# Both triangles multiplied in one slot, two vector products and one transpose queued behind the state's sums

## The chip, the cores and the metric

The kernel runs on one core of a Trainium2 chip. A core has a matrix engine (TensorE; PE in the profile, with PEld for its weight loads), a vector engine (VectorE, DVE), a scalar engine (ScalarE, ACT), GpSimd (POOL) and SyncE (SP), whose queue here issues most transfers. Each engine works through its own list of instructions in order, and semaphores hold one until what it needs is done. The metric is the time of one execution on the device in microseconds.

## The reference, cut to what matters

Three stages follow each other: a recurrence over 768 steps for 4 x 8 heads of width 40, a plain two-layer network, and a mixture of 8 experts.

```python
for t in range(S):                                   # S = 768
    y[:, :, t] = einsum('bhd,bhde->bhe', rt, state)
    Sa = einsum('bhde,bhe->bhd', state, at)
    state = state * wt - outer(Sa, bt) + outer(vt, kt)
x = y as (3072, 320)
g = relu(x @ w_in) ** 2;  x = g @ w_out              # w_in 320 x 2048
expert = argmax(x @ w_gate)                          # 8 experts, capacity 768 each
out = gate * (relu(x_e @ w1_e) @ w2_e) put back by token
```

## The kernel before

The 768 steps are cut into 12 stages of 64 steps (`NS`), and each stage into two chunks of 32 steps (`NC`, c = 0 and 1). Within a chunk nothing is done step by step: the products of the chunk's rows of `a` with its columns of `k` and `b` form two lower triangles per head, one of them is inverted, and with the inverse the 32 steps become matrix products.

What is needed of a stage before the state reaches it is made one stage ahead:

- `scale` loads `w`, `k` and `b` (tile `kb_d`, one buffer) and `a`; a scan over the decays gives R (`rq_r`, L115), `k` and `b` are multiplied by it on DVE (L146, two instructions), a second scan (`rq_q`, L128) gives what `a` is multiplied with on POOL (L280, through `times`). `kb_d` can be loaded anew only when both `lower` calls have read it.
- `lower(s, c)` multiplies the triangles of chunk c on PE (tile `pa`, 64 small products), copies one out on ACT (`solve_ab`, L174), masks the other on DVE (`am`, L176) and turns it into place in `a` (L180).
- `invert` transposes `solve_ab` of both chunks into `solve_al` on DVE (L187). Then POOL inverts by elimination: a memset, two copies, and 31 pairs of a product into `tmp` and a difference in `solve_tl`, all L280, each waiting for the one before it. `inverted` transposes the result back (`solve_tf`, L207) and forms `tt` (L210, L211).
- `steps` runs the same two scans with another layout (`wl`); `over` (L122, ACT) reads that R, and its transposed pieces `rt` (L244, L245, two buffers, one for each chunk) are fetched by SP as `rx` (L265), with which `zk` is multiplied.

In a stage, chunk c does in turn: `right` (tile `pr`: `a` times the state `zv`), `solve` (tile `psa`: the inverse `tt` times that), `turn` and `inner` (`psd`, `ppq`), `mix` (`ppq` masked into `lr`, L369), and the state's sums: `step` adds the products `pn` to `zv` and `other` adds the products of the chunk before to `zk` (both in `update`, L296, on DVE). `zk` of the chunk before is finally multiplied by the decay `g_b` (L389), before `out` (tile `py`) reads it.

The plain network's products (`pl` L434, `acc` L616) and its elementwise work (`g`, `gh`, `gl`) for the tokens already finished are put between these, a fixed number of pieces after each slot. The experts' products follow the recurrence (`upl`, `uacc`).

The program is recorded slot by slot, and a scheduler then sets each engine's order. Products on PE are kept in the order in which they were recorded (`keep_in_program_order`); on DVE, ACT and SP the scheduler moves instructions freely where no dependence or `issue_after` forbids it. Slots of chunk 0 are a to g, of chunk 1 a, b, d, f, g. Before, the two triangles of the next stage stand in different slots, with the network's pieces and slot d between them:

```python
def slot_c():
    if more: rw.lower(s + 1, 0)
def slot_e():
    if more:
        rw.lower(s + 1, 1)
        rw.invert(s + 1)
        st = rw.steps(s + 1)
```

Of the kernel before, what the change touches and what calls it, by code (L numbers as in the profile page):

```python
# [16 lines left out]
ALU = mybir.AluOpType  # L17
# [20 lines left out]
ROWS = 64 + D  # L38
# [19 lines left out]
BY_COL = [slice((1 - j) * 64, (1 - j) * 64 + D) for j in range(2)]  # L58
# [3 lines left out]
class Rwkv:  # L62
# [6 lines left out]
    def __init__(self, ctx, tc, ps, consts, keep, wd, kb, ad, rv, wl, tok, rng):  # L69
        self.tc, self.nc, self.ps = tc, tc.nc, ps  # L70
        self.c = consts
        self.src = dict(wd=wd, kb=kb, ad=ad, rv=rv, wl=wl, tok=tok)
        nc = self.nc
        p1 = ctx.enter_context(tc.tile_pool(name="rw1", bufs=1))
        self.p = ctx.enter_context(tc.tile_pool(name="rwr", bufs=1))
        self.dram = ctx.enter_context(tc.tile_pool(name="rwdram", bufs=2, space=DRAM))
        self.sq = p1.tile([128, 16, SEG], F32, name="seed_q")
        self.w = keep.tile([128, 1 + 16 * SEG], F32, tag="w_d", name="w_d")
        self.kb = keep.tile([128, 2, 16, SC], F32, tag="kb_d", name="kb_d")
        self.gb = p1.tile([128, 16, D], F32, name="g_b")  # L80
# [12 lines left out]
        for t in (self.a[1][32:64, :, 1], *(t[32:64, 1] for t in self.zv + self.lr + self.zk), self.gb[32:64]):
            nc.gpsimd.memset(t, 0.0)
        for t in (self.zv[0], self.zk[0]):
            nc.gpsimd.memset(t[0:64, 1], 0.0)
            nc.gpsimd.memset(t[64:128, 0], 0.0)
        self.last = None
        self.pre, self.rt = {}, {}

    def psum(self, name):
# [31 lines left out]
    def scale(self, s):  # L133

        nc, src = self.nc, self.src
        w, kb, a = self.w, self.kb, self.a[s % 2]
        for j in range(2):
            nc.sync.dma_start(out=w[BY_COL[j]], in_=src["wd"][s, j])
        for j in range(2):
            nc.sync.dma_start(out=kb[BY_COL[j]], in_=src["kb"][s, j])  # L140

        pr = self.products(w, 16, ROWS, s)
        r = next(pr)
        yield
        for k in range(2):
            nc.vector.tensor_mul(kb[:ROWS, k], kb[:ROWS, k], r[:ROWS, :, 1:SEG])  # L146
            yield
        g = self.tile([128, 16], f"g64.{s}", 2)
        nc.vector.tensor_copy(g[:ROWS], r[:ROWS, :, 0])
        self.pre[s] = [g, [None] * NC, None]  # L150
        for j in range(2):
            nc.sync.dma_start(out=a[BY_COL[j], :, j].rearrange("p c n t -> p c (n t)"), in_=src["ad"][s, j])
        q = next(pr)
        yield
        for j in range(2):
            v = a[BY_COL[j], :, j]
            self.times(s == 0 and j == 0, out=v, in0=v, in1=q[BY_COL[j], :, 0:SC].rearrange("p n (c t) -> p c n t", c=NC))
        self.wl = self.tile([128, 1 + 10 * SEG], f"wl.{s}", 1)
        nc.sync.dma_start(out=self.wl, in_=src["wl"][s])
        yield  # L160
# [42 lines left out]
    def inverted(self, s):  # L203

        nc, tl = self.nc, self.tl
        tf = self.tile([128, C, 2, NC, H], f"solve.tf{s}", 2)
        nc.vector.transpose(out=tf.rearrange("p t u c h -> p (t u c h)"),  # L207
                            in_=tl[:, :, :, None].to_broadcast([128, C, C // 2, 2]))
        tt = self.tile([128, C, NC, H], f"tt.{s}", 2)
        nc.scalar.mul(tt, tf[:, :, 0], self.c["odd"][:, 0:1])  # L210
        i = nc.vector.scalar_tensor_tensor(out=tt, in0=tf[:, :, 1], scalar=self.c["odd"][:, 1:2], in1=tt,  # L211
                                           op0=ALU.mult, op1=ALU.add)
        self.pre[s][2] = tt
        return i.ins
# [33 lines left out]
    def fetch(self, s, c):  # L248
# [17 lines left out]
        for j in range(2):  # L266
            v = zk[BY_STEP[j], j].rearrange("p (h y) e -> p y h e", y=2)
            self.times(c == 1, out=v, in0=v, in1=rx[BY_STEP[j]])

    def times(self, fast, **k):  # L270

        if fast:
            self.nc.vector.tensor_tensor(op=ALU.mult, **k)
        else:
            self.pool(self.nc.gpsimd.tensor_tensor, op=ALU.mult, **k)
# [9 lines left out]
    def update(self, s, c, z, l, r, half):  # L285

        nc = self.nc
        pn = self.psum(f"pn{s}_{c}_{half}")[:, 0:8 * D].rearrange("p (n e) -> p n e", n=8)
        for n in range(8):
            i = half * 8 + n  # L290
            for j in range(2):
                rows = BY_STEP[j]
                self.mm(pn[BY_COL[j], n], lhsT=l[rows, j, i], rhs=r[rows, j, i], start=True, stop=True)
        for j in range(2):
            rows, ns = BY_COL[j], slice(half * 8, half * 8 + 8)
            nc.vector.tensor_tensor(out=z[c ^ 1][rows, j, ns], in0=z[c][rows, j, ns], in1=pn[rows], op=ALU.add)  # L296

    def right(self, s, c):

# [26 lines left out]

    def step(self, s, c, half):

        self.update(s, c, self.zv, self.zk[c], self.zv[c], half)

    def decay(self, s):

# [49 lines left out]

    def other(self, s, c, half):

        self.update(s, c, self.zk, self.zv[c], self.zk[c], half)
        if half == 1 and c == NC - 1 and s + 1 < NS:
            for j in range(2):
                v = self.zk[c ^ 1][BY_COL[j], j]
                self.nc.vector.tensor_mul(v, v, self.gb[BY_COL[j]])  # L389

# [930 lines left out]
def tile_rwkv__mlp__moe(ctx, tc, wd, kb, ad, rv, wl, tok, nat, w_in, w_out, w_gate, w1, w2, cap, cst1, cst2, out):  # L1323
    nc = tc.nc
# [8 lines left out]
    with ExitStack() as ph:  # L1333
# [4 lines left out]
        rw = Rwkv(rp, tc, ps, consts, keep, wd, kb, ad, rv, wl, tok, rng)  # L1338
# [48 lines left out]
        for s in range(NS):  # L1387
# [3 lines left out]
            for c in range(NC):  # L1391
                last, y = ys, None
# [25 lines left out]
                def slot_c():  # L1418
                    if s > 1:
                        pieces.append(ml.bursts(s - 1, xs.pop(s - 1)))  # L1420
                    if more:
                        rw.lower(s + 1, 0)

                def slot_d():
                    rw.turn(s, c)
                    rw.inner(s, c)

                def slot_e():
                    nonlocal st
                    if more:  # L1430
                        rw.lower(s + 1, 1)
                        rw.invert(s + 1)
                        st = rw.steps(s + 1)
                        next(st)

# [10 lines left out]
                def slot_g():  # L1446
                    rw.step(s, c, 0)
                    rw.step(s, c, 1)
                    if c == 1 and more:
                        rw.inverted(s + 1)  # L1450

                parts = slot_a, slot_b, slot_c, slot_d, slot_e, slot_f, slot_g
                if c == 1:
                    parts = slot_a, slot_b, slot_d, slot_f, slot_g
# [48 lines left out]
    n = nc.values_load(good[0:1, 0:1], min_val=0, max_val=128)  # L1503
# [86 lines left out]
```

## Time and profile before

| | us |
|---|---|
| median of 3 runs | 1195.83 (1195.64 to 1196.54) |
| the profiled execution | 1200.53 |
| its span in the trace | 1198.7 |
| recurrence, from the first chunk to the last sums | about 85 to 880 |
| experts | from about 880 to the end |

The profiled execution is one more execution, 4.70 us above the median; the trace covers its span, and 1.83 us lie around it. Times in the views are counted from the span's start. In a timeline row, square brackets give the engine's idle time just before the instruction and what ended it.

### The profile page before, as it was taken

How to read it: one execution, taken by the hardware profiler on the slowest of the kernel's cores; microseconds unless marked ns; L12 is line 12 of the kernel's file. 1: busy time of each engine (PE TensorE's matmuls, PEld its weight loads, DVE VectorE, ACT ScalarE, POOL GpSimd, SP SyncE). 2: the span in 40 equal slices, each digit the busy share in tenths (PEclk: the TensorE clock that was granted, in tenths of full speed). 3: DMA queues.
4: the chain of work that ended last, by engine and by line, in shares of the span. 5: the costliest groups of instructions: out<-in, count | busy, mean ns of one | idle time of the engine just before them, and what ended most of it. 6: DMA issues, size and time to landing. Idle time of an engine off the chain costs nothing.

```text
span 1198.7 us, 42394 instructions
## 1 busy us (share of the span) xinstructions
PE 969.2 (81%) x17749; PEld 901.3 (75%) x17749; DVE 915.0 (76%) x1925; ACT 491.7 (41%) x1301; POOL 570.5 (48%) x912
## 2 busy tenths in 40 slices
PE   1665446688989898979899797998989998999993
PEld 1554346677878787878788787887979998999993
DVE  8999887586878878686868788675867886777770
ACT  2443222233424232423324232342337475767760
POOL 5773936548283856648282847554000032222220
PEclk9999978898888888989989898999999999999997
DMA  8724524653343534343433535233267275767630
GB/s 243 201 80 132 153 57 108 232 141 116 102 122 102 132 104 125 107 132 107 131 116 86 132 104 141 87 118 92 86 193 245 77 238 183 218 198 223 219 95 8
DMA packets 87610, 164.37 MB, mean 137 GB/s; under 512 B 16313, under 2 KB 46651, under 8 KB 86444
## 3 DMA queue, kind: packets, MB, share of 16 engines
q1 hardware_dynamic: 78476, 141.47, 40.8%
q10 hardware_dynamic: 6048, 11.06, 3.2%
q0 software_dynamic: 2880, 8.98, 2.2%
q8 instruction: 143, 2.34, 0.8%
q14 instruction: 63, 0.52, 0.1%
HBM read 137.23 MB, written 16.29 MB: 128 GB/s over the span
## 4 chain that ended last, share of the span: by engine, by line
PE 29%; POOL 25%; DVE 20%; DMA 11%; issue 9%; ACT 4%; SPq 1%; POOLq 0%; ACTq 0%; DVEq 0%
POOL solve_tl L280 13%; POOL tmp L280 12%; PE upl L434 6%; PE uacc L1114 6%; PE acc L616 6%; PE pl L434 4%; DMA out_dram<-uo,room 2%; DVE zv L296 2%; DMA xg<-x_dram,room 2%; DVE gl L397 2%; DMA kb_d<-in_kb_dram 2%; DMA stage_hi<-in_w_out_dram 2%; DVE g L634 2%; DVE rq_r L115 1%; DVE solve_tf L207 1%
## 5 line engine op out<-in xcount | busy, mean ns | idle before, releaser
L280 POOL TENSOR_TENSOR solve_tl<-solve_tl,tmp 128x126 f32<-128x126 f32 (+22 forms) x372 | 195.0, 524 | 29.1
L280 POOL TENSOR_TENSOR tmp<-solve_al,solve_tl 128x126 f32<-128x126 f32 (+22 forms) x372 | 186.4, 501 | 33.1 <-DVE a L180 4.9
L616 PE MATMUL acc<-woh,gh 128*128 128x328 f32 x384 | 133.6, 348 | 12.9 <-ACT gh L396 12.7
L616 PE MATMUL acc<-woh,gl 128*128 128x328 f32 x384 | 130.1, 339 | 9.1 <-DVE gl L397 8.8
L616 PE MATMUL acc<-wol,gh 128*128 128x328 f32 x384 | 126.5, 329 | 0.0
L434 PE MATMUL pl<-x_hi,wi_hi 128*128 128x256 f32 x384 | 121.8, 317 | 1.7 <-ACT x_hi L446 1.7
L434 PE MATMUL pl<-x_lo,wi_hi 128*128 128x256 f32 x384 | 113.4, 295 | 11.0 <-DVE x_lo L449 11.0
L434 PE MATMUL pl<-x_hi,wi_lo 128*128 128x256 f32 x384 | 113.0, 294 | 0.0
L280 POOL MEMSET solve_tl<- 128x512 f32 x12 | 6.3, 527 | 215.4 <-DVE solve_al L187 215.4
L396 ACT CAST gh<-g 128x512 fp32r<-128x512 f32 x96 | 59.5, 620 | 120.2 <-DVE g L634 112.8
L1192 POOL DMA_INDIRECT out_dram<-uo,room x30 | 34.1, 1136 | 155.2 <-DVE uo L1181 84.1
L1122 POOL DMA_INDIRECT xg<-x_dram,room x30 | 30.4, 1012 | 141.6 <-DVE gl L397 61.4
L632 ACT ACTIVATE g<-pl 128x512 f32<-128x512 f32 x96 | 57.6, 600 | 97.2 <-PE pl L434 96.8
L397 DVE TENSOR_TENSOR gl<-g,gh 128x512 fp32r<-128x512 f32 x96 | 71.9, 749 | 26.4 <-ACT gh L396 26.3
L616 PEld LDWEIGHTS acc<-woh,gh 128*128 128x128 f32 x384 | 77.9, 203 | 17.0 <-ACT gh L396 13.3
L616 PEld LDWEIGHTS acc<-woh,gl 128*128 128x128 f32 x384 | 78.0, 203 | 15.3 <-DVE gl L397 14.6
L1114 PE MATMUL uacc<-w2h,hh 128*128 128x320 f32 x240 | 77.0, 321 | 12.0 <-ACT wi_hi L1070 12.0
L434 PEld LDWEIGHTS pl<-x_lo,wi_hi 128*128 128x128 f32 x384 | 78.1, 203 | 11.3 <-DVE x_lo L449 11.3
L283 PE MATMUL pr<-zv,a 104*32 104x40 f32 (+1 forms) x1536 | 44.0, 245 | 50.2 <-DVE zv L296 32.1
L434 PEld LDWEIGHTS pl<-x_hi,wi_hi 128*128 128x128 f32 x384 | 77.6, 202 | 6.5 <-ACT x_hi L446 2.1
L283 PEld LDWEIGHTS pr<-zv,a 104*32 104x32 f32 (+1 forms) x1536 | 31.7, 143 | 62.2 <-DVE zv L296 42.5
L616 PEld LDWEIGHTS acc<-wol,gh 128*128 128x128 f32 x384 | 78.2, 204 | 0.0
(272 smaller groups left out, 3030.6 us busy)
## 6 DMA issues: line engine op xcount, KB each, us to landing
wol<-wol SPq DMA_DIRECT2D x96, 328.0 KB
w<-in_w_dram SPq DMA_DIRECT2D x30, 640.0 KB
w<-in_w_dram SPq DMA_DIRECT2D x30, 512.0 KB
kb_d<-in_kb_dram SPq DMA_DIRECT2D x24, 320.0 KB
zv<-in_tok_dram SPq DMA_DIRECT2D x48, 160.0 KB
zk<-in_tok_dram SPq DMA_DIRECT2D x48, 160.0 KB
rx<-rt SPq DMA_DIRECT2D x192, 40.0 KB
w<-in_w_dram SPq DMA_DIRECT2D x30, 256.0 KB
```

Source lines behind the costliest of these rows:

```text
L280: self.last = f(*a, **k).ins
L283: self.tc.keep_in_program_order(self.nc.tensor.matmul(*a, **k))
L296: nc.vector.tensor_tensor(out=z[c ^ 1][rows, j, ns], in0=z[c][rows, j, ns], in1=pn[rows], op=ALU.add)
L396: return (nc.scalar.copy(hi, x).ins, nc.vector.tensor_tensor(out=lo, in0=x, in1=hi.bitcast(F32), op=ALU.subtract).ins)
L397: nc.vector.tensor_tensor(out=lo, in0=x, in1=hi.bitcast(F32), op=ALU.subtract).ins)
L434: tc.keep_in_program_order(tc.nc.tensor.matmul(out, lhsT=a, rhs=b, start=n == 0, stop=n == len(seq) - 1))
L616: self.tc.keep_in_program_order(self.nc.tensor.matmul(*a, **k))
L632: nc.scalar.activation(g, pl, AF.Relu)
L634: nc.vector.tensor_tensor(out=g, in0=pl, in1=g, op=ALU.mult)
L1114: self.tc.keep_in_program_order(self.nc.tensor.matmul(*a, **k))
L1122: nc.gpsimd.indirect_dma_start(out=xg[:, 0:DX], out_offset=None, in_=self.x1, in_offset=bass.IndirectOffsetOnAxis(ap=self.idx[2 * j + t], ...
L1192: self.nc.gpsimd.indirect_dma_start(out=self.out, out_offset=bass.IndirectOffsetOnAxis(ap=self.to[:, n:n + 1], axis=0), in_=o[:, t], in_of ...
```

## The change

`slot_c` now records both `lower` calls and `invert`; `slot_e` keeps `steps` alone. Two kinds of DVE instructions get an edge that keeps them behind others on DVE, without a semaphore: the products of `kb_d` with R stand behind the last recorded sums of `zv` (`self.sums[0]`) and of `zk` (`self.sums[1]`, with the product by `g_b` where there is one), and the transpose of the inverse stands behind the last sums of `zv`.

```diff
         for k in range(2):
-            nc.vector.tensor_mul(kb[:ROWS, k], kb[:ROWS, k], r[:ROWS, :, 1:SEG])
+            with self.behind(2):
+                nc.vector.tensor_mul(kb[:ROWS, k], kb[:ROWS, k], r[:ROWS, :, 1:SEG])
             yield
...
-        nc.vector.transpose(out=tf..., in_=tl...)
+        with self.behind(1):
+            nc.vector.transpose(out=tf..., in_=tl...)
...
+    def behind(self, n):
+        order = ExitStack()
+        for i in self.sums[:n]:
+            order.enter_context(self.tc.issue_after(i))
+        return order
...
     def step(self, s, c, half):
-        self.update(s, c, self.zv, self.zk[c], self.zv[c], half)
+        self.sums[:1] = [self.update(s, c, self.zv, self.zk[c], self.zv[c], half)]
...
     def other(self, s, c, half):
-        self.update(s, c, self.zk, self.zv[c], self.zk[c], half)
+        last = self.update(s, c, self.zk, self.zv[c], self.zk[c], half)
...
+                last = self.nc.vector.tensor_mul(v, v, self.gb[BY_COL[j]]).ins
+        self.sums[1:] = [last]
...
                 def slot_c():
                     if more:
                         rw.lower(s + 1, 0)
+                        rw.lower(s + 1, 1)
+                        rw.invert(s + 1)
                 def slot_e():
                     if more:
-                        rw.lower(s + 1, 1)
-                        rw.invert(s + 1)
                         st = rw.steps(s + 1)
```

On PE the 64 products of `pa_1` move up to directly behind those of `pa_0`; nothing else moves there. On SP the two loads of `kb_d` move up in front of the loads `wol_1`, `v_1` and `wol_2` and the stores of `x_dram`, and one of the two loads of `w_d` moves behind `v_0` and `wol_6`. POOL's order is the same. The larger part moves on DVE, shown for one stage in the middle of the recurrence (every stage from the fourth on has this pattern).

First place: DVE from the mask of the first triangle (`am_0`) to the transpose `solve_al` that POOL waits for. Before:

```order
L176 TENSOR_TENSOR am_0_7607<-pa_0_7572,ct 128x256
L115 SCALAR_TENSOR_TENSOR rq_r_8053<-w_d,seed_q 104x1040
L180 STREAM_TRANSPOSE a_116<-am_0_7607 64x8x32 x2
L124 TENSOR_SCALAR rq_r_8053<-rq_r_8053 104x1040
L125 RECIPROCAL seed_q<-rq_r_8053 104x16
L149 COPY g_8_8320<-rq_r_8053 104x16
L634 TENSOR_TENSOR g_0_7691<-pl_0_7621,g_0_7691 128x512
L664 COPY logits<-x_0_7710 128x8
L397 TENSOR_TENSOR gl_0_7695<-g_0_7691,gh_0_7694 128x512
L664 COPY logits<-x_1_7715 128x8
L176 TENSOR_TENSOR am_1_7755<-pa_1_7720,ct 128x256
L187 STREAM_TRANSPOSE solve_al_7761<-solve_ab_7571 128x1024
```

The same place in the changed kernel:

```order
L178 TENSOR_TENSOR am_0_7607<-pa_0_7572,ct 128x256
L113 MEMSET seed_q 104x16
L247 STREAM_TRANSPOSE qt_0_8516<-rq_q_8046 128x8x32
L248 STREAM_TRANSPOSE qt_0_8516<-rq_q_8046 128x8x8
L189 STREAM_TRANSPOSE solve_al_7654<-solve_ab_7571 128x1024
L182 STREAM_TRANSPOSE a_116<-am_0_7607 64x8x32 x2
L116 SCALAR_TENSOR_TENSOR rq_r_8053<-w_d,seed_q 104x1040
L178 TENSOR_TENSOR am_1_7648<-pa_1_7613,ct 128x256
L125 TENSOR_SCALAR rq_r_8053<-rq_r_8053 104x1040
L182 STREAM_TRANSPOSE a_116<-am_1_7648 64x8x32 x2
```

`solve_al` has moved from the eleventh place behind `am_0` to the fourth; the scan of `w_d`, the clamp of R and the network's pieces, which stood ahead of it, now follow it.

Second place: DVE in chunk 0, from the mask `lr` to the state's sums of `zv`. Before:

```order
L369 TENSOR_TENSOR lr_119<-ppq_0_7650,ct 64x512 x2
L296 TENSOR_TENSOR zk_121<-zk_122,pn_1_1_7899 40x320 x2
L397 TENSOR_TENSOR gl_1_7862<-g_1_7858,gh_1_7861 128x512
L146 TENSOR_TENSOR kb_d<-kb_d,rq_r_8053 104x1024 x2
L389 TENSOR_TENSOR zk_121<-zk_121,g_b 40x640 x2
L273 TENSOR_TENSOR zk_122<-zk_122,rx_1_7931 64x2x8x40
L296 TENSOR_TENSOR zv_118<-zv_117,pn_0_0_7967 40x320 x2
L273 TENSOR_TENSOR zk_122<-zk_122,rx_1_7931 64x2x8x40
L296 TENSOR_TENSOR zv_118<-zv_117,pn_0_1_7986 40x320 x2
L128 SCALAR_TENSOR_TENSOR rq_q_8324<-w_d,seed_q 104x1040
```

In the changed kernel:

```order
L380 TENSOR_TENSOR lr_119<-ppq_0_7760,ct 64x512 x2
L306 TENSOR_TENSOR zk_121<-zk_122,pn_1_1_7899 40x320 x2
L409 TENSOR_TENSOR gl_1_7862<-g_1_7858,gh_1_7861 128x512
L400 TENSOR_TENSOR zk_121<-zk_121,g_b 40x640 x2
L283 TENSOR_TENSOR zk_122<-zk_122,rx_1_7931 64x2x8x40
L306 TENSOR_TENSOR zv_118<-zv_117,pn_0_0_7967 40x320 x2
L283 TENSOR_TENSOR zk_122<-zk_122,rx_1_7931 64x2x8x40
L306 TENSOR_TENSOR zv_118<-zv_117,pn_0_1_7986 40x320 x2
L148 TENSOR_TENSOR kb_d<-kb_d,rq_r_8053 104x1024
```

The two products of `kb_d` have left the place ahead of the product by `g_b`; the first stands behind the sums of `zv`, the second (not in these rows) in chunk 1, behind the sums of `zk` with `pn_0_0`.

Third place: DVE in chunk 1, from the network's piece `g_4` to the transpose of the inverse. Before:

```order
L634 TENSOR_TENSOR g_4_8254<-pl_4_8237,g_4_8254 128x512
L397 TENSOR_TENSOR gl_4_8258<-g_4_8254,gh_4_8257 128x512
L369 TENSOR_TENSOR lr_120<-ppq_1_8287,ct 64x512 x2
L207 STREAM_TRANSPOSE solve_tf_8479<-solve_tl_7763 128x1024
L296 TENSOR_TENSOR zk_122<-zk_121,pn_0_1_8377 40x320 x2
L634 TENSOR_TENSOR g_5_8428<-pl_5_8334,g_5_8428 128x512
L211 SCALAR_TENSOR_TENSOR tt_8481<-solve_tf_8479,ct,tt_8481 128x512
L296 TENSOR_TENSOR zv_117<-zv_118,pn_1_0_8441 40x320 x2
L296 TENSOR_TENSOR zv_117<-zv_118,pn_1_1_8460 40x320 x2
```

In the changed kernel:

```order
L646 TENSOR_TENSOR g_4_8254<-pl_4_8237,g_4_8254 128x512
L129 SCALAR_TENSOR_TENSOR rq_q_8324<-w_d,seed_q 104x1040
L409 TENSOR_TENSOR gl_4_8258<-g_4_8254,gh_4_8257 128x512
L113 MEMSET seed_q 128x10
L116 SCALAR_TENSOR_TENSOR rq_r_8969<-wl_8418,seed_q 128x650
L380 TENSOR_TENSOR lr_120<-ppq_1_8287,ct 64x512 x2
L306 TENSOR_TENSOR zk_122<-zk_121,pn_0_1_8377 40x320 x2
L646 TENSOR_TENSOR g_5_8428<-pl_5_8334,g_5_8428 128x512
L306 TENSOR_TENSOR zv_117<-zv_118,pn_1_0_8441 40x320 x2
L409 TENSOR_TENSOR gl_5_8432<-g_5_8428,gh_5_8431 128x512
L306 TENSOR_TENSOR zv_117<-zv_118,pn_1_1_8460 40x320 x2
L210 STREAM_TRANSPOSE solve_tf_8479<-solve_tl_7656 128x1024
```

The transpose `solve_tf`, which stood ahead of all sums with `pn_0_1`, `pn_1_0` and `pn_1_1`, now follows them; the two scans, which stood in chunk 0, now stand ahead of the mask `lr`.

## Rows read from the trace of the kernel before

**Rows 1.** The page's first part: busy time, share, instructions of each engine.

```profile
PE 969.2 (81%) x17749; PEld 901.3 (75%) x17749; DVE 915.0 (76%) x1925; ACT 491.7 (41%) x1301; POOL 570.5 (48%) x912
```

**Rows 2.** Windows: one middle stage; its length, busy by engine, clock, DMA share.

```profile
504.00:570.00 66.00, 57.25 (x1319) 52.05 (x1319) 51.17 (x87) 22.82 (x52) 40.39 (x69) 0.89 0.42 117
```

**Rows 3.** The waits: engine, line, for whom; total us, times, longest.

```profile
DVE solve_tf L207 <- POOL solve_tl L280: 57.5, 11, 9.9
DVE kb_d L146 <- DMA kb_d<-in_kb_dram: 26.4, 12, 2.9
```

**Rows 4.** PE's timeline: start, length; chunk 0's psa 7 stages apart, one stage between.

```profile
305.85 1.16 PE L283 MATMUL psa<-rh,tt 32*32 32x40 f32 x64
...
503.92 1.14 PE L283 MATMUL psa<-rh,tt 32*32 32x40 f32 x64
...
508.74 1.10 PE L283 MATMUL pa<-kb_d,a 40*32 40x64 f32 x64
...
516.47 1.10 PE L283 MATMUL pa<-kb_d,a 40*32 40x64 f32 x64
...
533.39 0.31 PE L283 MATMUL py<-zk,lr 104*32 104x40 f32 x2 [4.09 <-DVE zk L389]
...
544.57 1.12 PE L283 MATMUL psa<-rh,tt 32*32 32x40 f32 x64
```

**Rows 5.** DVE's timeline in chunk 0 of that stage: the products of kb, a scan.

```profile
529.75 2.56 DVE L146 TENSOR_TENSOR kb_d<-kb_d,rq_r 104x1024 f32<-104x1024 f32 x2 [2.52 <-DMA kb_d<-in_kb_dram]
...
537.77 2.31 DVE L128 TENSOR_TENSOR_SCAN rq_q<-w_d,seed_q 104x1040 f32<-104x1040 f32 x1
```

**Rows 6.** Windows of 3 us behind that wait; the columns of rows 2.

```profile
535.00:538.00 3.00, 2.02 (x72) 1.40 (x67) 2.88 (x6) 0.00 (x0) 2.61 (x6) 0.50 0.32 96
538.00:541.00 3.00, 3.00 (x41) 2.91 (x42) 3.00 (x3) 0.73 (x2) 2.84 (x3) 0.50 0.23 70
```

**Rows 7.** DVE's timeline: chunk 1's mask, the inverse's transpose in three stages.

```profile
494.06 1.25 DVE L207 STREAM_TRANSPOSE solve_tf<-solve_tl 128x1024 f32<-128x1024 f32 x1 [3.38 <-POOL solve_tl L280]
...
553.91 1.39 DVE L369 TENSOR_TENSOR lr<-ppq,ct 64x512 f32<-64x512 f32 x2 [2.58 <-PE ppq L283]
560.05 1.25 DVE L207 STREAM_TRANSPOSE solve_tf<-solve_tl 128x1024 f32<-128x1024 f32 x1 [4.75 <-POOL solve_tl L280]
...
820.97 1.25 DVE L207 STREAM_TRANSPOSE solve_tf<-solve_tl 128x1024 f32<-128x1024 f32 x1 [5.40 <-POOL solve_tl L280]
```

**Rows 8.** PE's timeline: psa in the last stage, which loads and multiplies no kb.

```profile
770.77 1.12 PE L283 MATMUL psa<-rh,tt 32*32 32x40 f32 x64
...
802.96 1.12 PE L283 MATMUL psa<-rh,tt 32*32 32x40 f32 x64
...
829.70 1.12 PE L283 MATMUL psa<-rh,tt 32*32 32x40 f32 x64
```

**Rows 9.** DVE's timeline from rt's second piece to solve_al (21 rows), four of them.

```profile
509.40 0.45 DVE L244 STREAM_TRANSPOSE rt<-rq_r 128x256 f32<-128x256 f32 x1 [1.19 <-DMA rx<-rt]
...
514.86 2.30 DVE L115 TENSOR_TENSOR_SCAN rq_r<-w_d,seed_q 104x1040 f32<-104x1040 f32 x1
...
518.00 0.70 DVE L124 TENSOR_SCALAR rq_r<-rq_r 104x1040 f32<-104x1040 f32 x1
...
521.67 1.24 DVE L187 STREAM_TRANSPOSE solve_al<-solve_ab 128x1024 f32<-128x1024 f32 x1
```

**Rows 10.** SP's timeline: the queue around the second half of rx's transfers.

```profile
503.38 0.36 SPq L620 DMA_DIRECT2D wol<-wol  x1
503.78 4.12 SPq L265 DMA_DIRECT2D rx<-rt  x5
```

**Rows 11.** Windows, POOL alone: the inversion in a middle and the last stage.

```profile
523.05:560.05 37.00, 32.16 (x66) 0.86 0.51 136
788.53:820.97 32.44, 27.45 (x66) 1.00 0.42 125
```

**Rows 12.** POOL's timeline: the same product beside the scan, and in the last stage.

```profile
537.67 2.60 POOL L280 TENSOR_TENSOR tmp<-solve_al,solve_tl 128x120 f32<-128x120 f32 x1
...
802.15 0.40 POOL L280 TENSOR_TENSOR tmp<-solve_al,solve_tl 128x120 f32<-128x120 f32 x1
```

More of the change, by code (lines that the diff above doesn't have):

```diff
@@ L98, in __init__ @@
         self.last = None
+        self.sums = []
         self.pre, self.rt = {}, {}
@@ L206, in inverted @@
         tf = self.tile([128, C, 2, NC, H], f"solve.tf{s}", 2)
-        nc.vector.transpose(out=tf.rearrange("p t u c h -> p (t u c h)"),
-                            in_=tl[:, :, :, None].to_broadcast([128, C, C // 2, 2]))
+        with self.behind(1):
+            nc.vector.transpose(out=tf.rearrange("p t u c h -> p (t u c h)"),
+                                in_=tl[:, :, :, None].to_broadcast([128, C, C // 2, 2]))
         tt = self.tile([128, C, NC, H], f"tt.{s}", 2)
@@ L295, in update @@
             rows, ns = BY_COL[j], slice(half * 8, half * 8 + 8)
-            nc.vector.tensor_tensor(out=z[c ^ 1][rows, j, ns], in0=z[c][rows, j, ns], in1=pn[rows], op=ALU.add)
+            i = nc.vector.tensor_tensor(out=z[c ^ 1][rows, j, ns], in0=z[c][rows, j, ns], in1=pn[rows], op=ALU.add)
+        return i.ins
     def right(self, s, c):
@@ L388, in other @@
                 v = self.zk[c ^ 1][BY_COL[j], j]
-                self.nc.vector.tensor_mul(v, v, self.gb[BY_COL[j]])
+                last = self.nc.vector.tensor_mul(v, v, self.gb[BY_COL[j]]).ins
+        self.sums[1:] = [last]
 def split(nc, hi, lo, x):
```

## The prediction

> **What bounds the kernel now.** I read the busy shares first. No engine is full: the matrix engine is busy 81% and the vector engine 76% of the span [rows 1], and one middle stage of the recurrence shows the same, 57.25 and 51.17 us of 66.00, POOL 40.39 [rows 2]. So a stage is set by waits, and I looked for the ones that recur once a stage. The list of waits has two on the vector engine that answer to the change: for POOL's inversion, 57.5 us in 11 stages, and for the load of kb, 26.4 us in 12 [rows 3]. The timelines then give a stage's length. From chunk 0's psa at 305.85 to the one at 770.77 there are seven stages, 464.92 / 7 = 66.4 us each [rows 4, 8]. A stage has two halves: psa of chunk 0 to psa of chunk 1, 544.57 - 503.92 = 40.65 us [rows 4], and the rest, 66.4 - 40.65 = 25.75 us.
>
> In the first half the vector engine stands 2.52 us for kb's load and multiplies for 2.56 us before it gets to the product by g_b [rows 5]; PE's py waits 4.09 us for just that product [rows 4]. Behind this wait PE's granted clock is 0.50, its lower level of 1.2 GHz, for the next windows [rows 6]. In the second half the vector engine stands 4.75 us in front of the inverse's transpose with the state's sums queued behind it [rows 7], and PE's pr needs those sums.
>
> Two things run round once a stage. The state's way is psa, sums, pr, psa. The inverse's way is POOL's inversion (37.0 us [rows 11]), then the product of zk with rx on POOL, over, the transfers of rx (5 of 8 behind one wol on SP [rows 10]), the second rt transpose, which waits for these transfers [rows 9], and from there the vector engine's queue down to solve_al, which starts POOL again. Whichever is longer after the change sets the stage.
>
> **The state's way, part by part.** First half: with kb's two products behind the sums, the wait of 2.52 and the 2.56 us of work leave the path to g_b, 5.1 us [rows 5]. The load starts after pa_1, which moves from 516.47 to right behind pa_0 at 508.74, 516.47 - 508.74 - 1.10 = 6.6 us sooner [rows 4], and its products stand later in the queue, so I cost its landing at nothing; what hides it is the whole of the sums. If the cover is gone, it costs at most the wait of today, 2.52. The clock: in the 6 us of rows 6 PE works 5.0 us at 0.50, which is half as much at full clock; with a gap of 4.09 us gone I count 2 of the 2.5 us as returned. So 40.65 - 5.1 - 2 = 33.6 us. A row bounds it from below: the last stage has no kb and none of the scans, and its first half is 802.96 - 770.77 = 32.19 us [rows 8]; from above 40.65 - 5.1 = 35.6, the clock staying low.
>
> Second half: the wait of 4.75 and the transpose's 1.25 us leave the path in front of the sums [rows 7], 6.0 us. Added ahead of the mask lr are the second kb product (half of 2.56), the scan that gives rq_q (2.31) [rows 5], and the scan of wl, which no row here shows and which lies below the 2.30 us of the wider scan of w_d [rows 9]; at 1.7 by its width, 650 of 1040 elements and a little, this is 5.3 us. The mask waits 2.58 us for PE today [rows 7], which hides that much; two waits of the network's pieces hide perhaps 1 more. Net 1.7 later, between 0 (all hidden behind PE) and 5.3 (nothing hidden). So 25.75 - 6.0 + 1.7 = 21.5 us, with 20 and 25 as ends. The state's way alone would run at 33.6 + 21.5 = 55 us a stage. The last stage with its 5.40 us of waiting for the inverse taken out is 829.70 - 770.77 - 5.40 = 53.5 [rows 7, 8], near it.
>
> **The inverse's way.** Before, from the end of POOL's inversion (494.06, where the vector engine's wait ends [rows 7]) to the second rt transpose at 509.40 are 15.3 us; from there to the end of solve_al, 521.67 + 1.24 - 509.40 = 13.5 us [rows 9]; the inversion 37.0 and some handover: 66. The order's first place says what stands between rt and solve_al in the changed kernel: the same rows up to am_0 without the network's g, then the short transposes, then solve_al. The scan of w_d and everything up to am_1 falls behind it. Before, that stretch ran from 514.86 to 521.67 [rows 9]: 6.8 of the 13.5 us go, and 6.7 stay. In exchange the scan lies beside the inversion. What that costs POOL a row shows: a product of 120 elements takes 2.60 us beside the rq_q scan and 0.40 in the last stage [rows 12], so 2.2 us for a scan. The whole inversion takes 32.4 us in the last stage, without scans and kb, against 37.0 [rows 11]. I take 37.0 + 2.2 = 39.2; the ends are 34.5 (kb's products slide out of it, one scan in) and 41 (all in, and the clamp too). The way round is 15.3 + 6.7 + 39.2 = 61.2. Of the 15.3 some is a wait of SP's wol load, issued at 503.38 with five rx transfers behind it [rows 10]; it waits for PE, and PE comes sooner, so I give back 1 us: 60. Ends 55 and 63.
>
> Here the Trainium skill speaks against the change: SBUF — State Buffer, section "Who interferes with whom", says that a tensor_scalar of the vector engine can enter a two-port mode and then holds the port pair that it shares with GpSimd for the whole instruction, though it has one input only. The clamp of R is such an instruction and also moves into the inversion. No row of the kernel before has it there, so the trace does not show it; by that rule the inversion would be some 0.7 us longer, as an estimate from the clamp's 0.70 us [rows 9], and the stage 60.7.
>
> The inverse's way is then the longer one, 60 against 55, and the stage loses 6.4 us. The wait for the inverse does not vanish on PE but moves from pr to psa, which needs tt.
>
> **The sum.** Seven stages are timed by rows 4 and 8, two more before them have the same build and the same two waits: 9 x 6.4 = 57.6 us. The stage that begins at 770.77 has no kb; its solve_al comes sooner, and of its 5.40 us [rows 7] I count 4. The first stage, in which the vector engine still prepares weights, I count at nothing, and the experts behind the recurrence too: their instructions are untouched and only start sooner. 1200.53 - 61.6 = 1138.9 us for the profiled execution. That one ran 4.70 us above the median of the runs shown, so the forecast is 1138.9 - 4.7 = 1134.2, say 1134 us. With the stage between 58 and 62 (of 9 x 8.4 + 5 and 9 x 4.4 + 2) it is 1115 to 1154.
>
> **The rivals.**
> *The inverse's way is shorter than I think*, because kb's products leave the inversion and the rx transfers come as PE does; the state's way decides at 55. Then 9 x 11.4 + 5 = 108 us, 1088. For it: the last stage's 53.5; against: the scan has to go somewhere, and rows 12 show its price. Chance 0.13.
>
> *A new wait takes the place*, on the vector engine ahead of lr: all 5.3 us of scans and product come late, the clock falls there instead (state's way 35.6 + 25 = 60.6), and PE's delay is handed on through the wol load to rx and rt, so that the inverse's way comes to 63 or 64. A stage loses 2.9: 9 x 2.9 + 2 = 28, 1168. For it: the vector engine is at 51.17 us of work, and 60 leaves it little slack for waits that stay. Chance 0.21.
>
> *Slower.* The scan for rq_q now lies in chunk 1, and the loads of w_d that wait for it stand on SP ahead of v_0, wol_6 and the loads of zv and zk for the next chunk. If the scan slips by 8 us, zv's rows land after pr wants them; that wait, the 2.5 us of clock behind it [rows 6] and the 5.3 us of scans stand against 5.1 + 6.0 = 11.1 us that go: it decides from 3.3 us late on. At twice py's wait of today, 8.2 us [rows 4], a stage gains 8.2 + 2.5 + 5.3 - 11.1 = 4.9 us, and the time is 1195.8 + 9 x 4.9 = 1240. Against it: SP has gaps today, and the scan's slip by the order is about 2 us past the wait of lr. Chance 0.04.
>
> *It does nothing*: the edges are orders without a wait, and if POOL's inversion, stretched by what now runs beside it, ends as late as before relative to the sums, solve_tf only waits in another place. Time 1196. Against it: solve_al starts 6.8 us sooner and the stretch known is 2.2. Chance 0.02.
>
> **How the numbers follow.** My case has 0.60 and its own range 1115 to 1154. Below it lies the first rival at 1088, above it the second at 1168. The range that leaves 2 in 10 out cuts most of the first and all of the last two: 1103 to 1176. Under 0.2% (2.4 us, about what measurements of this kernel tell from no change) lies next to nothing of the first three cases: same 0.02. Slower 0.04, faster 0.94.
>
> **What would show it.** Right: the stage between two psa of chunk 0 near 60 us; kb's wait of 2.5 us gone from the vector engine; py's wait for g_b under 1 us and no window at clock 0.50 behind it; pa_1 right behind pa_0 and solve_al some 6.6 us behind rt; the inversion near 39 us; solve_tf still with a short wait or none, and no sums queued behind it. The first rival is right if the inversion is under 36 us and the stage at 55; the second if lr has no wait, POOL idles as before and the stage is at 63. Wrong altogether: pr waiting for the zv load, or w_d's load holding SP.

## The result, and the profile after

| | before | after |
|---|---|---|
| median of 4 runs, us | 1195.74 (1193.28 to 1196.54) | 1163.92 (1160.67 to 1166.40) |
| profiled execution, us | 1200.53 | 1164.89 |
| mean stage, fifth solve_tf to eleventh, us | (760.46 - 362.14) / 6 = 66.4 | (733.47 - 352.35) / 6 = 63.5 |

The ratio is 0.9721, 95% interval 0.9688 to 0.9755: 2.8% faster. The forecast was 1134 us; 31.8 us were won where 61.6 were expected, and 2.9 us of a stage where 6.4 were. One of the four executions of e9 below came out at 1279.34 us at a granted clock of 0.67 (0.92 to 0.93 in the others) and is in neither its median nor its ratio.

The first lines are the busy shares of the page, one middle stage (columns as in [rows 2]) and four lines of the list of waits (total, times, longest).

```profile
PE 947.6 (81%) x17749; PEld 889.1 (76%) x17749; DVE 935.7 (80%) x1925; ACT 490.0 (42%) x1301; POOL 602.2 (52%) x912
```

```profile
479.20:542.60 63.40, 53.79 (x1315) 49.86 (x1316) 54.18 (x86) 22.68 (x52) 44.36 (x70) 0.92 0.42 121
```

```profile
DVE solve_tf L210 <- POOL solve_tl L290: 42.9, 9, 6.3
...
PE acc L628 <- ACT gh L408: 30.6, 10, 5.1
...
PE pt L453 <- DVE y L390: 25.9, 11, 7.9
...
POOL tmp L290 <- DVE a L182: 20.0, 11, 2.6
```

Against [rows 2] DVE does 54.18 us of work in 63.4, before 51.17 in 66.0, though nothing was added to it: some of its instructions have become longer. POOL too: 44.36, before 40.39. Of [rows 3] the wait for kb is down from 26.4 us in 12 stages to 4.0 in two early ones; solve_tf still waits 42.9 (57.5). POOL's wait for am's transpose has come to nearly every stage (20.0 in 11, before 4.9 in 2), and PE's wait for gh has grown from 12.7 to 30.6. PE's wait for y has grown most, from 1.8 to 25.9: y stands on DVE behind solve_tf, so this is the wait for the inverse, which PE now meets in front of psa, as forecast.

One stage on DVE, from the end of POOL's inversion to the next (start, duration, wait in brackets):

```profile
479.14 1.25 DVE L210 STREAM_TRANSPOSE solve_tf<-solve_tl 128x1024 f32<-128x1024 f32 x1 [4.42 <-POOL solve_tl L290]
...
482.79 5.43 DVE L348 TENSOR_TENSOR zv<-zv,g 40x640 f32<-40x640 f32 x2
...
493.31 0.43 DVE L247 STREAM_TRANSPOSE rt<-rq_r 128x256 f32<-128x256 f32 x1
...
498.38 1.20 DVE L189 STREAM_TRANSPOSE solve_al<-solve_ab 128x1024 f32<-128x1024 f32 x1
...
500.41 2.33 DVE L116 TENSOR_TENSOR_SCAN rq_r<-w_d,seed_q 104x1040 f32<-104x1040 f32 x1
...
503.57 0.90 DVE L182 STREAM_TRANSPOSE a<-am 64x256 f32<-64x256 f32 x2
...
505.57 0.69 DVE L646 TENSOR_TENSOR g<-pl,g 128x512 f32<-128x512 f32 x1 [0.78 <-ACT g L644]
...
516.68 1.21 DVE L148 TENSOR_TENSOR kb_d<-kb_d,rq_r 104x1024 f32<-104x1024 f32 x1
...
528.22 2.32 DVE L129 TENSOR_TENSOR_SCAN rq_q<-w_d,seed_q 104x1040 f32<-104x1040 f32 x1
```

And POOL in the same stage, from the end of one inversion to the end of the next:

```profile
478.88 0.22 POOL L290 TENSOR_TENSOR solve_tl<-solve_tl,tmp 128x16 f32<-128x16 f32 x1
...
482.18 5.36 POOL L290 TENSOR_TENSOR a<-a,rq_q 40x1024 f32<-40x1024 f32 x2
499.70 0.53 POOL L290 MEMSET solve_tl<- 128x512 f32 x1 [12.16 <-DVE solve_al L189]
500.29 2.45 POOL L290 COPY solve_tl<-ct 128x16 f32<-128x16 f32 x2
504.62 0.25 POOL L290 TENSOR_TENSOR tmp<-solve_al,solve_tl 128x31 f32<-128x31 f32 x1 [1.88 <-DVE a L182]
...
528.44 2.93 POOL L290 TENSOR_TENSOR tmp<-solve_al,solve_tl 128x120 f32<-128x120 f32 x1
...
542.36 0.22 POOL L290 TENSOR_TENSOR solve_tl<-solve_tl,tmp 128x16 f32<-128x16 f32 x1
```

This is the inverse's way, and it closes on itself: POOL's end at 479.10 to rt at 493.31 is 14.2 us, rt to the end of solve_al at 499.58 is 6.3, the inversion from 499.70 to 542.58 is 42.9 with 0.1 of handover, 63.5 in all. The first two are the forecast's 14.3 and 6.7. The inversion is not: 42.9 where it had 39.2.

Before, DVE's clamp of the R of wl stood beside POOL's a times Q (497.15 to 502.42) and zv times g behind it:

```profile
501.26 1.52 DVE L124 TENSOR_SCALAR rq_r<-rq_r 128x650 f32<-128x650 f32 x1
502.81 1.67 DVE L337 TENSOR_TENSOR zv<-zv,g 40x640 f32<-40x640 f32 x2
```

After, the two have changed places: zv times g stands beside a times Q and takes 5.43 us, and the clamp behind it takes 0.48.

PE in the first half of the stage, and two 3 us windows over its gap (columns as in [rows 2], the last but two the granted clock):

```profile
485.02 1.29 PE L293 MATMUL psa<-rh,tt 32*32 32x40 f32 x64 [0.67 <-ACT rh L318]
...
506.96 0.41 PE L628 MATMUL acc<-woh,gh 128*128 128x328 f32 x1 [3.25 <-ACT gh L408]
...
516.21 0.80 PE L293 MATMUL py<-zk,lr 104*32 104x40 f32 x64
...
522.45 1.12 PE L293 MATMUL psa<-rh,tt 32*32 32x40 f32 x64
```

```profile
504.00:507.00 3.00, 0.04 (x1) 0.04 (x1) 1.55 (x7) 2.44 (x6) 1.90 (x7) 1.00 0.22 78
507.00:510.00 3.00, 2.69 (x9) 2.46 (x10) 2.99 (x6) 1.36 (x3) 2.46 (x7) 0.54 0.53 127
```

py's wait of 4.09 us [rows 4] is gone, but a gap of 3.25 us has come 9 us ahead of it, and the clock behind it falls to 0.54 as it fell to 0.50 in [rows 6]. What PE waits for there is gh, which needs DVE's g at 505.57. DVE itself stands 0.78 us for ACT's g, and that stands on ACT behind a copy of a:

```profile
504.04 0.88 ACT L183 COPY a<-a 64x256 f32<-64x256 f32 x2 [2.01 <-DVE a L182]
504.94 0.60 ACT L644 ACTIVATE g<-pl 128x512 f32<-128x512 f32 x1
```

The copy waits for am's second transpose, at 503.57 on DVE, which stands there behind the w_d scan and the clamp: the rows that the moved block pushed back.

### The profile page after: what moved, and what is told of

It reads as the page before. It is cut to its first block, busy times and chain, and to the rows that moved or that the text cites. A ratio compares the mean times of both kernels' runs of the same rounds, so it can differ in the third digit from the quotient of the medians.

```text
span 1163.1 us, 42377 instructions
## 1 busy us (share of the span) xinstructions
PE 947.6 (81%) x17749; PEld 889.1 (76%) x17749; DVE 935.7 (80%) x1925; ACT 490.0 (42%) x1301; POOL 602.2 (52%) x912
## 5 line engine op out<-in xcount | busy, mean ns | idle before, releaser
L290 POOL TENSOR_TENSOR solve_tl<-solve_tl,tmp 128x126 f32<-128x126 f32 (+22 forms) x372 | 203.8, 548 | 29.2
L290 POOL TENSOR_TENSOR tmp<-solve_al,solve_tl 128x126 f32<-128x126 f32 (+22 forms) x372 | 192.2, 517 | 48.2 <-DVE a L182 20.0
L628 PE MATMUL acc<-woh,gh 128*128 128x328 f32 x384 | 134.2, 350 | 31.3 <-ACT gh L408 30.6
L646 DVE TENSOR_TENSOR g<-pl,g 128x512 f32<-128x512 f32 x96 | 65.6, 683 | 22.6 <-ACT g L644 21.6
L290 POOL MEMSET solve_tl<- 128x512 f32 x12 | 6.3, 527 | 138.7 <-DVE solve_al L189 138.7
L446 PEld LDWEIGHTS pl<-x_hi,wi_lo 128*128 128x128 f32 x384 | 77.5, 202 | 0.0
```

The source lines that it names most:

```text
L290: self.last = f(*a, **k).ins
L446: tc.keep_in_program_order(tc.nc.tensor.matmul(out, lhsT=a, rhs=b, start=n == 0, stop=n == len(seq) - 1))
L628: self.tc.keep_in_program_order(self.nc.tensor.matmul(*a, **k))
L646: nc.vector.tensor_tensor(out=g, in0=pl, in1=g, op=ALU.mult)
```

## The experiments

Each run is set against runs of the kernel before that were made with it; their medians are 1196 to 1204 us, so ratios are compared. The times in the expectations are meant beside the 1195.74 us of the result: a ratio times that is what compares with them. "Stage" is the mean of the six from the fifth solve_tf to the eleventh.

| run | what is different from the kernel after | median us | ratio to before (95%) | stage |
|---|---|---|---|---|
| after | | 1163.92 | 0.9721 (0.9688 to 0.9755) | 63.5 |
| e1_slot_only | neither queueing | 1221.24 | 1.0164 (1.0098 to 1.0229) | 67.8 |
| e2_edges_only | second block back in its slot | 1183.18 | 0.9827 (0.9763 to 0.9891) | 65.7 |
| e12_slot_tf | kb not queued | 1178.36 | 0.9790 (0.9738 to 0.9841) | 63.1 |
| e3_own_tmp | tmp in its own buffer | 1155.35 | 0.9613 (0.9554 to 0.9673) | 61.7 |
| e5_own_tl | tmp and solve_tl in their own | 1142.73 | 0.9555 (0.9518 to 0.9592) | 61.8 |
| e4_aq_dve | a times Q on DVE | 1183.28 | 0.9852 (0.9789 to 0.9915) | 64.1 |
| e6_aq_late | e3, a times Q to follow zv times g (did not) | 1154.98 | 0.9642 (0.9608 to 0.9675) | 62.0 |
| e7_aq_rt | e6, three buffers for rt | 1150.20 | 0.9621 (0.9586 to 0.9656) | 61.1 |
| e9_aq_held | e3, a times Q behind zv times g | 1150.48 | 0.9601 (0.9536 to 0.9665) | 61.8 |
| e10_tl_held | e5 and e9 | 1144.34 | 0.9567 (0.9511 to 0.9623) | 61.6 |
| e8_no_qscan | Q's scan of w_d left out | 1143.03 | 0.9547 (0.9510 to 0.9585) | 61.9 |
| e11_short_inv | e3, 18 of 31 inversion steps | 1136.22 | 0.9461 (0.9411 to 0.9512) | 61.2 |

### The change taken apart: e1, e2, e12

```diff
e1:  -  with self.behind(2):  (k and b times R)     -  with self.behind(1):  (solve_tf)
e2:  slot_c  -  rw.lower(s + 1, 1); rw.invert(s + 1)      slot_e  +  the same
e12: -  with self.behind(2):  (k and b times R)
```

> The changed kernel with both blocks of triangles in the third slot, but k and b times R and the inverse's transpose free to be placed ahead of the state's sums, as in the kernel before. Theory 1 (the loop through GpSimd sets the stage: GpSimd's end, VectorE's queue to rt, solve_al, the inversion, 63.5 us in the changed kernel): only what this adds to VectorE's queue between GpSimd's end and rt counts, the two zv sums that stand behind solve_tf again, about 2 us of a stage; time 1175 to 1185. Theory 2 (the state's way through VectorE and TensorE sets it): the kb wait of 2.5 us comes back and solve_tf's 4.4 us are in that way again, 6 us or more of a stage; 1210 or more, above the kernel before.

> The changed kernel with the second block of triangles and the inversion's start back in the fifth slot; the two queueings stay. Theory 1 (the loop through GpSimd): its 13.5 us from rt to solve_al come back, of which the kernel before had the same; the queueings take only the sums out of the piece behind GpSimd's end: a stage of 65 to 66 us, 1180 to 1195. Theory 2 (the state's way): the two waits of 2.5 and 4.4 to 4.75 us were what the change won, and most of it stays: 1155 to 1170, as the changed kernel.

> The changed kernel with only k and b times R set free again; the inverse's transpose stays queued behind the state's sums. It tells which of the two queueings the change needs. If the transpose's place carries them (in the run with neither, solve_tf waited 7 to 9 us with the sums behind it): 1160 to 1175, near the changed kernel. If k and b times R carry as much (their wait for the load, 2.5 us of a stage, ahead of lr): 1180 to 1195.

The block's move alone is slower than the kernel before, by 1.0 to 2.3%; the queueings alone win 1.7%; together they win 2.8%. So the parts do not add up. e1's time is the one that the second theory gave (by ratio 1215 us); e2's stage is the one of the first, while its time (by ratio 1175 us) lies between the two. DVE of e1 shows why the move alone loses:

```profile
505.91 1.25 DVE L209 STREAM_TRANSPOSE solve_tf<-solve_tl 128x1024 f32<-128x1024 f32 x1 [7.27 <-POOL solve_tl L289]
...
508.62 1.39 DVE L379 TENSOR_TENSOR lr<-ppq,ct 64x512 f32<-64x512 f32 x2
509.92 1.00 DVE L305 TENSOR_TENSOR zk<-zk,pn 40x320 f32<-40x320 f32 x2
...
511.55 1.00 DVE L305 TENSOR_TENSOR zv<-zv,pn 40x320 f32<-40x320 f32 x2
```

Here the scheduler has put solve_tf ahead of lr and of all the sums; DVE stands 7.27 us with the state's work behind it. As I read these rows, the inversion then lies inside the state's way, and both ways add up instead of running side by side. e12 bears this out: queueing solve_tf alone brings the stage from 67.8 to 63.1, as in the kernel after. In e12 k and b times R are back in one piece ahead of the rq_q scan, and wait for nothing, while solve_tf waits 0.72 us in this stage:

```profile
516.49 2.33 DVE L147 TENSOR_TENSOR kb_d<-kb_d,rq_r 104x1024 f32<-104x1024 f32 x2
...
553.76 1.25 DVE L209 STREAM_TRANSPOSE solve_tf<-solve_tl 128x1024 f32<-128x1024 f32 x1 [0.72 <-POOL solve_tl L289]
```

The wait for kb's load is nearly gone with either half of the change: 4.1 us in 4 waits in e1, which has the move alone, 6.1 in 3 in e2, which has the queueing alone, and 3.8 in 4 here, against 26.4 in 12 before. What the queueing of k and b's products adds to e12 is in the first stages: e12's fifth solve_tf is at 364.45, the one of after at 352.35, 12 us sooner. By ratio e12's time is 1171 us, in its first range.

### The terms of the inversion: e3, e5, e8, e4

```diff
e3:  -  tmp = self.tile([128, 144], f"tmp.{s}", 1, tag="am")
     +  tmp = self.tile([128, 144], f"tmp.{s}", 1)
e5:  e3 and  -  tl = self.tile([128, C, C // 2], f"solve.tl{s}", 2)
             +  tl = self.tile([128, C, C // 2], f"solve.tl{s}", 1, tag="tl")
e8:  products, n == 16:  +  yield r; return   (ahead of Q's scan)
e4:  a times Q:  -  self.times(s == 0 and j == 0, ...)   +  self.times(s > 1 or j == 0 and s == 0, ...)
```

> The changed kernel with a buffer of its own for the inversion's product tmp, which shared one with the masked triangles am and waited 1.88 us at the inversion's first product for the last transpose of am. Theory 1 (the loop through GpSimd sets the stage): 1.9 us of each of some 9 stages, 17 us: 1143 to 1152, stage 61.6. Theory 2 (VectorE's and TensorE's way sets it): 1162 to 1166, stage 63.5, with a longer wait of GpSimd elsewhere.

> The changed kernel with tmp in a buffer of its own and the inversion's solve_tl too, which had shared two buffers with solve_ab, solve_al and solve_tf, so that its clearing and two copies (0.53 and 2.45 us, the latter beside the w_d scan) could begin only behind solve_al. Theory 1 (loop through GpSimd, VectorE's two-input instructions hold GpSimd for their length): the three go ahead of solve_al into GpSimd's idle time, but the scan, 2.3 us, then holds the first product, so only their own 1.0 us goes: stage 60.6 (61.6 with tmp alone), 1145. Theory 2 (the scan costs only beside these copies): 3.1 us of each stage, 58.5, 1127. Theory 3 (the loop no longer decides below 61.6): no change from 1155.

> The changed kernel without the scan that gives Q of w_d (a is multiplied by R in its place, so this part of the result is not computed); buffers as in the changed kernel. Beside that scan of 2.3 us one product of the inversion took 2.93 us in place of 0.39. Theory 1 (a scan on VectorE holds GpSimd, and the inversion is in the loop): the stage loses 2.5 us, 61.0, 1142. Theory 2 (the inversion is not in the loop, or is held by something else than the scan): 1160 to 1166.

> The changed kernel with a times Q multiplied on VectorE behind its scan, not on GpSimd behind the inversion. VectorE gets two instructions of about 1.3 us (estimated from the two of zv times g, 1.67 us together, by their elements) at a place where it waits for nothing of the loop; GpSimd loses 5.4 us. Theory 1 (the loop): zv times g, 5.43 us beside it now, is back at 1.7, rt comes 3 to 3.8 us earlier, and the stage is 60: 1128 to 1142. Theory 2 (VectorE's queue, 54 of 63.5 us busy, is the bound): 2.6 us more of VectorE, less what zv times g gives back: 1160 to 1190.

POOL's first rows of the inversion in e3, and then in e5 with the clearing and copies of the same inversion:

```profile
490.48 2.45 POOL L290 COPY solve_tl<-ct 128x16 f32<-128x16 f32 x2
492.88 0.23 POOL L290 TENSOR_TENSOR tmp<-solve_al,solve_tl 128x31 f32<-128x31 f32 x1
493.19 0.79 POOL L290 TENSOR_TENSOR solve_tl<-solve_tl,tmp 128x31 f32<-128x31 f32 x1
```

```profile
476.30 0.52 POOL L290 MEMSET solve_tl<- 128x512 f32 x1
476.88 0.34 POOL L290 COPY solve_tl<-ct 128x16 f32<-128x16 f32 x2
...
486.30 0.24 POOL L290 TENSOR_TENSOR tmp<-solve_al,solve_tl 128x31 f32<-128x31 f32 x1 [9.09 <-DVE solve_al L189]
486.62 0.27 POOL L290 TENSOR_TENSOR solve_tl<-solve_tl,tmp 128x31 f32<-128x31 f32 x1
...
487.29 2.16 POOL L290 TENSOR_TENSOR solve_tl<-solve_tl,tmp 128x30 f32<-128x30 f32 x1
```

In e3 the wait of 1.88 is gone and the stage is 1.9 shorter, within 0.1 of what the first theory gave (and by ratio 1149 us, in its range): the inverse's way sets the stage of the kernel after. In e5 the two copies take 0.34 us in place of 2.45, and the scan instead stretches a difference of 30 elements to 2.16 us: it costs about its length here too. The stages of 60.6 that were expected do occur in e5 (from 404.78 to 465.38 on POOL, for one), but others are 63 to 64 and the mean is 61.8. Those follow a solve_tf that no longer waits, so something else ends last there. Its ratio is nevertheless the lowest of the complete kernels, 0.9555, though the intervals of e3, e9 and e10 overlap with its; it lies clear below that of after, so this version beats both kernels. In e8 the inversion of the stage at 484.86 takes 36.06 us from its first product to its end, 37.96 in the kernel after. Its time is the first theory's, but its stage is 1.6 shorter, not 2.5: the rest was won in the first stages (fifth solve_tf at 335.93, after 352.35).

e4 took the expected 3.8 us off zv times g and still became slower than after; by ratio 1178 us, its time is in the second theory's range. Its rows on DVE, the first three behind POOL's end at 488.39, the last at the rq_q scan:

```profile
492.08 1.67 DVE L348 TENSOR_TENSOR zv<-zv,g 40x640 f32<-40x640 f32 x2
...
499.91 0.69 DVE L646 TENSOR_TENSOR g<-pl,g 128x512 f32<-128x512 f32 x1 [1.45 <-ACT g L644]
501.56 0.45 DVE L247 STREAM_TRANSPOSE rt<-rq_r 128x256 f32<-128x256 f32 x1 [0.96 <-DMA rx<-rt]
...
539.63 2.66 DVE L283 TENSOR_TENSOR a<-a,rq_q 40x1024 f32<-40x1024 f32 x2
```

Of the 3.8 us, 2.8 come back as waits (0.37 and 1.45 for PE's products through ACT, 0.96 for the transfers of rx), so rt is 13.2 us behind POOL's end, not 14.2 - 3.8 = 10.4; and a times Q now stretches the inversion, which takes 39.48 us from its first product in place of 37.96. DVE's work as such is not what sets e4's stage: solve_tf still waits 3.91 us for POOL in it, at 488.42.

### Past the inverse's way: e6, e7, e9, e10, e11

```diff
e6:  e3 and  +  yield; yield; yield   (a times Q recorded later, the load of wl ahead of it)
             +  with self.tc.issue_after(self.held): nc.vector.tensor_copy(v, v)   # v = a[0:1, 0, 0, 0, 0:1]
e7:  e6 and  -  f"rt.{s}_{c}", 2)   +  f"rt.{s}_{c}", 3)
e9:  as e6 with  v = a[64:65, 0, 0, 0, 0:1]          e10: e9 with e5's buffers
e11: e3 and  -  for j in range(C - 1):   +  for j in range(18):
```

> The changed kernel with tmp in its own buffer, and a times Q on GpSimd made to wait for VectorE's zv times g (by a copy of one element of a onto itself behind it), so that the two no longer run side by side. zv times g, 5.43 us, is back at 1.67, and VectorE comes to the rows behind it 3.8 us earlier. Theory 1 (as the run with a times Q on VectorE showed: rt_1 then waits for the transfers of rx out of its buffer): only about 1 us of each stage, 60.6, 1146. Theory 2 (the 3.8 us were the loop's): 57.8, 1121.

> The one before with three buffers for rt in place of two, so that rt_1 waits for no transfer; the w_d scan thereby comes to stand ahead of solve_al, where GpSimd is idle, and no longer beside the inversion's first copies. Theory 1 (loop through GpSimd): 2.1 us of the copies and 2.8 us of the wait go, up to 3.0 us (scan and clamp) come into VectorE's queue ahead of solve_al: a stage of 58 to 59.5, 1122 to 1136. Theory 2 (the way of the state through VectorE and TensorE decides from about 60 us on): 60 to 61, 1140 to 1150.

> The kernel with tmp in its own buffer, and a times Q on GpSimd held behind zv times g. The earlier run meant for this copied an element that a times Q does not touch, so both still ran side by side; here the copied element lies in the rows of the first of the two. zv times g should take 1.67 us in place of 5.43. Theory 1 (rt_1 then waits for the transfers of rx, as with a times Q on VectorE): about 1 us of each stage of 61.6: 60.6, 1146. Theory 2 (the 3.8 us were the loop's): 57.8, 1121. Theory 3 (the state's way is at 61 already, as stages without a wait of solve_tf showed once solve_tl had its own buffer): 61 to 61.6, 1150 to 1156.

> Both: tmp and solve_tl in buffers of their own, and a times Q held behind zv times g. Theory 1 (loop through GpSimd): another 1 us of each stage, 59.6, 1134 to 1138. Theory 3 (the state's way decides from 61 us on): as the run with solve_tl in its own buffer, 61, 1140 to 1146, with no wait of solve_tf in most stages.

> The kernel with tmp in its own buffer and only the first 18 of the inversion's 31 steps (the rest of the inverse is not computed): GpSimd ends some 15 us earlier, so its loop, 61.6 us, falls to about 46 and cannot set the stage; what is left is the way of the state through VectorE and TensorE by itself. Theory 1 (that way is as short as the prediction had it): 55 to 57 us a stage, 1085 to 1105. Theory 3 (it is at 61 already): 59.5 to 61.5, 1135 to 1155, with no wait of solve_tf.

e6 failed as an experiment: the copied element is one that a times Q does not touch, so both ran side by side as before and its time repeats e3's. In e9 the hold works, on DVE and on POOL:

```profile
476.14 1.67 DVE L356 TENSOR_TENSOR zv<-zv,g 40x640 f32<-40x640 f32 x2
...
478.62 2.48 DVE L126 TENSOR_SCALAR rq_r<-rq_r 128x650 f32<-128x650 f32 x1
```

```profile
478.06 5.11 POOL L298 TENSOR_TENSOR a<-a,rq_q 40x1024 f32<-40x1024 f32 x2 [2.51 <-DVE a L166]
```

zv times g is at 1.67, and the next to be held is the clamp of R, 2.48 us in place of 0.48. e7, e9 and e10 all stay at 61.1 to 61.8 whatever they take off the inverse's way, as the theories of a limit by the state's way had it, to within 0.6; of e10's further 1 us nothing is seen. e11 shows the reason. With the inversion cut short, DVE and PE read (psa of chunk 0, chunk 1, chunk 0):

```profile
448.87 1.23 DVE L210 STREAM_TRANSPOSE solve_tf<-solve_tl 128x1024 f32<-128x1024 f32 x1
```

```profile
456.79 1.16 PE L293 MATMUL psa<-rh,tt 32*32 32x40 f32 x64 [0.81 <-ACT rh L318]
...
493.05 1.12 PE L293 MATMUL psa<-rh,tt 32*32 32x40 f32 x64
...
517.33 1.29 PE L293 MATMUL psa<-rh,tt 32*32 32x40 f32 x64 [0.66 <-ACT rh L318]
```

solve_tf waits for nothing (POOL had ended at 435.80, 13 us before), and a stage is still 61.2 us: 36.3 + 24.3 in this one. That is what is left when the inversion sets nothing. It is not the state's way in full purity: POOL's a times Q still stretches zv times g to 4.80 us here, in place of 1.67. Even if all of these 3.1 us lay in the state's way, it would have 58.1 by itself (my estimate, 61.2 less 3.1); it was forecast at 55, and the run rules that out.

## Why the forecast was right in kind and half in size

- **Where the time fell.** 1163.92 us lie inside the wide range (1103 to 1176) and outside the forecast's own case (1115 to 1154), and a stage of 63.5 lies above its upper end of 62. That the wide range holds is owed to the second rival, not to the sum.
- **The direction and the two waits.** kb's wait is gone, py's wait and the low clock behind it too, solve_al ends 6.3 us behind rt (6.7 forecast), the sums no longer stand behind solve_tf. That two ways race, and that the inverse's is the longer one, holds: e3 shortens that way by 1.9 and the stage follows by 1.9.
- **"I take 37.0 + 2.2 = 39.2" for the inversion is the first step that failed**: it takes 42.9, above the forecast's upper end of 41. The scan cost what was said: the copies take 2.45 us, 0.34 alone in e5, so 2.1. What was missed is 1.9 for tmp, which shares a buffer with am. The order's rows showed am's transpose falling behind scan and clamp, and solve_al was all I looked for there; the buffer that both use is not in the order. The other 1.9 is the chain of products itself, 38.0 us from its first product against 36.1 before. Each longer row has a two-input DVE instruction beside it: the forecast took the 37.0 as it stood. The moves put k and b's products beside two rows apart (1.64 and 1.78 us, where the pair cost rows of 1.21 and 1.24 before), the rq_q scan fully onto one product (2.93 us, 2.60 in [rows 12]), and gl with the last sums of zv into the chain (1.09 us for a difference of 96 elements that took 0.39 before).
- **"The state's way alone would run at 33.6 + 21.5 = 55" is the second**: e11 has 61.2. In the first half 33.6 counted kb's 5.1 us and 2 us of clock as returned; g's delay behind the moved scan opened a new gap of 3.25 us on PE, with the clock down again, and after has 522.45 - 485.02 = 37.4 us there, e11 36.3. In the second half the sum gave 1.7 us to scans and products that had moved in; e11 measures 24.3, 2.8 more, near the upper end of 25. The stage's own check, the last stage at 53.5, misled: that stage has no work for the next one. No run takes these terms apart one by one, so how much of the miss each of them is stays open.
- **What each miss is worth.** The stage is the longer of the two ways. With the floor of e11 at 61.2 (no run here came below 61.1), no shorter inversion could have given 60; by that floor 2.3 us of the 3.5 us missed in a stage are the inverse's way, 1.2 the state's. Six stages give 17.2 us, the stages before them 9.8 (fifth solve_tf 362.14 to 352.35), the last stage 1.8 where 4 were counted, and what follows the last solve_tf, which the forecast counted at nothing, 6.8 in these two executions, that of before having stood 4.7 above its median.
- **The rival that named "a new wait" had the better numbers** (stage 63 to 64, 1168 us; state's way 60.6): lr has no wait any more, and the clock falls in another place. But its road for the delay, through SP's transfers to rt, is not what the rows show: rt waits less for transfers after the change (2.0 us in 3 stages, 10.8 in 7 before; none in the stage shown), and POOL waits less for solve_al, not as long as before (138.7 us in 12 stages, 215.4 before). The state's way does not decide at 63.5; the inversion does.
- **The 14.3 us from POOL's end to rt came out for another reason.** The forecast tied them to transfers; after, it is zv times g, 5.43 us beside POOL's a times Q against 1.67 before. So the sum came out right here by luck. e4 and e9 take the 3.8 us away, and the transfers are next: rt then waits 0.96 and 0.67 us for rx, and is only 1.0 and 0.7 us sooner.
- **The clamp.** In e3 the clamp lies beside the first difference of 31 elements, which takes 0.79 us, and 0.27 in e5 where it does not: 0.5 us. In e9 it is the other way round, and the clamp waits for POOL. The Trainium skill (SBUF — State Buffer, "Who interferes with whom") says of the port pair that the two engines share that whoever issues first has it for the whole instruction while the other blocks; the traces agree in both directions, with the clamp 0.03 us ahead of the difference in e3 and 0.56 us behind a times Q in e9. The prediction's estimate of 0.7 us came near. It held that no row of before shows such a clamp inside the inversion; but the trace of before did show a clamp held by POOL, the 1.52 us at 501.26. In the kernel after it cost nothing, since POOL was still waiting for am.

## What to carry to other kernels

When two chains share a queue, starting the slow one sooner is worth something only if its result is also taken later than the other chain's work; here the first half alone cost 1.6% and both together won 2.8%. Before a block is moved, look up what shares a buffer with each of its tiles: the order of instructions does not show it, and one line (a buffer of its own, e3) gave back 1.9 of 63.5 us. And work out the second-longest way as carefully as the longest, by leaving out the longest in a run if need be: it is the floor under every gain.

## What was not expected of the hardware

- DVE's scans, with two inputs in SBUF and 2.3 us long, stretched GpSimd's instruction beside them by 1.9 to 2.5 us, wherever in the chain they fell: 2.45 us for two copies that take 0.34 alone, 2.16 for a difference that otherwise took 0.26 (e3's row of that shape), 2.93 for a product that took 0.40 in [rows 12].
- It works against DVE as strongly: zv times g took 5.43 us in place of 1.67 while GpSimd's a times Q, begun 0.61 us before, took 5.36, against 5.11 behind it in e9. In e5 at 468.49 zv times g began 1.35 us before a times Q: then it took 4.79 us, and a times Q 6.51.
- An instruction with one SBUF input is held too: the clamp, 2.48 us in place of 0.48, when a times Q had begun 0.56 us before.
- Not settled: why single stages of e5, e9 and e10 alternate between about 60 and 64 us. e11's do so as well (59.1 to 64.8), so the inversion is not needed for it; in its longest stage, from 508.68, DVE waits 2.24 us for rx and 1.57 us for the load of zk, against 0.56 and nothing in the stage before. Nor is it settled what each term of the 61.2 us is; no run took its parts away one by one.
